# State-space rows kept in the natural order of channels, with two stores a unit

## The chip, the cores and the metric

The kernel runs on one core of one Trainium2 chip. The metric is the device time of one execution in microseconds (us). The core has five engines with queues of their own: TensorE (PE) for matrix products, ScalarE (ACT) for exponentials, VectorE (DVE) for element-wise work, GpSimd (POOL), and SyncE (SP), which in this kernel issues nearly all the transfers between DRAM and the on-chip memory (SBUF). TensorE writes its results into a small memory of its own, PSUM.

## What is computed

Two branches read the same `x` (2048 positions by 512 channels) and are mixed position by position by a gate:

```python
g = sigmoid((x * gate_w).sum(-1, keepdims=True))
# a: attention, 32 heads of 16 channels
qkv = (x @ wqkv) -> q, k, v
p = softmax(q @ k.T * 16 ** -0.5)          # 32 heads, 2048 x 2048 each
a = (p @ v) @ wo
# b: a state-space convolution, one filter of 2048 taps for each channel
dt = exp(log_dt); A = A_re + 1j * A_im
P = exp(dt * A * l)                         # 512 channels x 128 states x 2048 taps
K = einsum("dn,dnl,dn->dl", C, P, dt * B).real
b = causal_convolution(x, K) + x * Dskip
return g * a + (1 - g) * b
```

Inputs and output are 16-bit floats.

## The kernel before, in words

**Attention.** The scores of one head, 128 keys by 512 queries, make one tile; there are 2048 tiles. Three tiles are made at a time by matmuls into one of two PSUM buffers (`SC`). ACT takes the exponential of two or three of them (line 907) into `ET`. In some groups one tile is left to DVE, which makes an approximate exponential with integer arithmetic: four such tiles (`bits`, line 943, buffer `DZ`) and three more passes (`batch`, line 954, `DZ` and `DU`) make one "set". The products with `v` gather in the PSUM buffer `OA`; `norm_a`, `norm_b` and `norm_c` transpose and divide them on DVE (lines 978 to 997). There are 32 blocks of 64 tiles.

**State space.** The convolution is done in chunks of 64 positions. Filter tables are made on DVE, a scan over the chunks runs on DVE in two halves of the channels (`scan`, lines 1331 to 1342), and `ystage` makes the output. It works through 32 units of 16 channels, units 0 to 15 after the first half of the scan, 16 to 31 after the second. The channels are held in an order in which channel d stands next to channel d + 256. A unit adds up in the PSUM buffer `MB`, with four column strips (j) by four groups (q): one product of the scan's states with `Py`, one of the inputs `XY` with the short filters `Tt`. Four strips of 32 chunks of 64 positions lie on the 128 partitions, so one partition strip holds one channel of each group q. The DVE multiplies the sum by the gate into `Yst` (line 1415, four buffers in turn), and SP stores it to the DRAM tensor `ytd` with one transfer (line 1420). After every second unit `yread` (line 1433) is queued: a transposing transfer of 32 channel rows by 2048 positions from `ytd` into `Yl`, in which position lies on the partitions and the 512 channels, in the kernel's own order, in the row. `yloads` brings `Py` and `Tt` for up to three units ahead, again on SP.

**The final sums.** Of the 16 row groups of 128 positions, 12 have their attention part finished early (`early`), put out to DRAM and read back (`reload`, line 1556) into three buffers `AR`. `outs` waits for all the reads of `Yl` and then adds `Yl` to each `AR` on DVE, four row groups at a time (line 1565), stores the result (line 1567), and loads `Wo` once more. The last four row groups are done behind the last block: `ident` brings `Yl` into PSUM by a product with the identity matrix, `out_mm` adds the attention part to it, ACT or DVE copies the sum out, and it is stored. In `outs` and in `ident` the access patterns turn the kernel's order of channels into the natural one:

```python
PERM, NAT = [[1, 2], [2, 256]], [[256, 2], [1, 256]]
```

`PERM` reads two half rows, each with steps of two elements; `NAT` is the matching view of the natural order.

**What sets the order.** The order of instructions is made in Python before the kernel is built. `Sched` keeps a set of threads (generators) with priorities; each yields an engine and a cost, and `fill` picks, step by step, what is ready first by modelled times: every operation has a cost `c` and a delay `lat` in microseconds, and a reader of a transfer keeps a further margin of 2.4 (`DMARG`). `decide` chooses while this runs which score tiles go to DVE, from the modelled idle time of ACT and DVE and from whether the buffers of an earlier set are free; three windows of group numbers (`WIN`) say where this may be. So a changed cost or a further transfer changes the order of everything planned behind it. Every engine's queue is then carried out in that order, with waits on semaphores. `place` gives buffers their addresses by the stretches in which they live. Matmuls by a zero matrix (`wm`) are put in to keep TensorE busy (`FILL`).

Of the kernel before, what the change touches and what calls it, by code (L numbers as in the profile page):

```python
# [11 lines left out]
ALU = mybir.AluOpType  # L12

P = 128
S = 2048
D = 512
NH = 32
DH = 16
T = 64
NCH = S // T  # L20
NBLK = 16
CB = D // NBLK
# [65 lines left out]
class Prog:  # L88
# [133 lines left out]
    def dma(self, eng, fn, R=(), W=(), c=.45, lat=3.0, m=DMARG):  # L222
        if self.cap is not None:
            self.cap.append((self.dma, (eng, fn, R, W), dict(c=c, lat=lat, m=m)))
            return
        self.log.append((self.dma, self.q, (eng, fn, R, W)))
        k = self.dnext
        self.dnext = (k + 1) % NDSEM
        s = ("D", k)
        deps = self._deps(s, R, W)  # L230
        if self.dn[k]:
            deps[s] = max(deps.get(s, -1), self.dn[k])
        at = self.tm[eng]
        for s2, k2 in deps.items():
            at = max(at, self.fin[(s2, k2)] + .08)
        self.tm[eng] = at + c
        self.dn[k] += 1
        self.fin[(s, self.dn[k])] = at + c + lat
        self.marg[(s, self.dn[k])] = m
        self._record(eng, fn, deps, s, self.dn[k], R, W)  # L240
# [369 lines left out]
def record(nc, p, B, ins):  # L610
# [5 lines left out]
    sch = Sched(p)  # L616
    op, dma = p.op, p.dma
# [6 lines left out]
    def mm(out, lhsT, rhs, R, W, start=True, stop=True, pos=None, c=MM, a=512, cfg="F"):  # L624
        kw = {} if pos is None else dict(tile_position=pos)
        op("PE", lambda t: t.matmul(out(), lhsT(), rhs(), start=start, stop=stop, skip_group_check=True, **kw), R, W,  # L626
           c=c, lat=.15, a=a, cfg=cfg)
# [47 lines left out]
    idf, idb, x0n = B["idf"], B["idb"], B["x0n"]  # L675
# [334 lines left out]
    PERM, NAT = [[1, 2], [2, 256]], [[256, 2], [1, 256]]  # L1010
# [341 lines left out]
    Py, Tt, Yst, ytd, Yl = B["Py"], B["Tt"], B["Yst"], B["ytd"], B["Yl"]  # L1352
# [26 lines left out]
    def ystage():  # L1379
        def unit(u):  # L1380
            blk, hf = divmod(u, 2)
            qr, bl = divmod(blk, 4)
            sg, h, k8 = SG[qr // 2], qr // 2, blk % 8
            r, r2 = u % 3, u % 4
            yield ("AFTER", f"scan{h}")
            yield ("AFTER", "gt")
            yield ("AFTER", f"yl{u}")
            yield ("AFTER", f"xy{qr}")
            yield ("LOCK", "MB")
            ky = [(MB, 0, ('y', u))]  # L1390
            yield ("PE", .12)
            for j in range(4):
                mm(lambda j=j: MB(0, [[1, 256]], 32 * j, 32), lambda: wm(0, [[1, 32]]), lambda: wm(0, [[1, 256]]), [(wm, 0)], ky, True, False,
                   pos=(0, 32 * j), c=.11 if j == 0 else 0, a=64, cfg="C")
            for q in range(4):
                yield ("PE", .15)
                for ri in range(2):
                    for j in range(4):
                        i = 4 * q + j
                        mm(lambda q=q, j=j: MB(64 * q, [[1, 64]], 32 * j, 32),  # L1400
                           lambda ri=ri, i=i: sg(ri * SGH + CB * k8 + 16 * hf + 8 * (i % 2) + i // 2, [[2 * SGH, 32]]),
                           lambda ri=ri, i=i: Py(r * YN + ri * 16 * T + i * T, [[1, T]]),
                           [(sg, b_, (h, 'G')) for b_ in range(32)] + [(sg, "z"), (Py, r, u)], ky, False, False,
                           pos=(0, 32 * j), c=.075 if j == 0 else 0, a=16, cfg="C")
            for q in range(4):
                yield ("PE", .09)
                for j in range(4):
                    par, k = j % 2, 2 * q + j // 2
                    mm(lambda q=q, j=j: MB(64 * q, [[1, 64]], 32 * j, 32),
                       lambda k=k, par=par: B[f"XY{qr}"](16 * bl + 8 * hf + k, [[64, 32]], 64 * par, 64),  # L1410
                       lambda k=k, par=par: Tt(r * 512 + 64 * k, [[1, 64]], 64 * par, 64),
                       [(B[f"XY{qr}"], par), (Tt, (r, par, k // 4), u)], ky, False, True, pos=(64 * par, 32 * j), c=.085 if j == 0 else 0, a=8,
                       cfg="H")
            yield ("DVE", .4, -1)
            op("DVE", lambda v: v.tensor_tensor(Yst(r2 * 256, [[64, 4], [1, 64]]), MB(0, [[64, 4], [1, 64]]), B["gt"](0, [[0, 4], [1, 64]]),
                                                ALU.mult), ky + [(B["gt"], j) for j in range(4)], [(Yst, r2, u)], c=.37)
            sch.unlock("MB")
            sch.mark(f"yu{u}")
            yield ("SP", .45)
            dma("SP", lambda e: e.dma_start(ytd.dram(16 * u * S, [[T, P], [4 * S, 4], [1, T]]), Yst(r2 * 256, [[64, 4], [1, 64]])),  # L1420
                [(Yst, r2, u)], [(ytd, u)], c=.6, lat=3.2)
            if hf == 1:
                if bl == 3:
                    sch.mark(f"yq{qr}")
                sch.add(yread(blk), 3)

        for u in range(2 * NBLK):
            yield from unit(u)

    def yread(blk):  # L1430
        yield ("AFTER", "yu15")
        yield ("SP", 1.2)
        dma("SP", lambda e: e.dma_start_transpose(Yl(CB * blk, [[D, 16], [1, CB]]), ytd.dram(CB * blk * S, [[S, CB], [1, S]])),
            [(ytd, 2 * blk), (ytd, 2 * blk + 1)], [(Yl, blk)], c=1.26, lat=1.6)
        sch.mark(f"yr{blk}")


    def xload(b, qr):
# [120 lines left out]
    def outs():  # L1559
        for blk in range(NBLK):  # L1560
            yield ("AFTER", f"yr{blk}")
        for qc in range(3):
            AO = B[f"AR{qc}"]
            yield ("DVE", 2.3, 0)
            op("DVE", lambda v, qc=qc, AO=AO: v.tensor_tensor(AO(0, [[D, 4]] + NAT), AO(0, [[D, 4]] + NAT), Yl(4 * D * qc, [[D, 4]] + PERM), ALU.add),  # L1565
               [(AO, r, "a") for r in range(4)] + [(Yl, x) for x in range(NBLK)], [(AO, r, "y") for r in range(4)], c=2.2)
            later("SP", .5, 3, lambda qc=qc, AO=AO: dma("SP", lambda e: e.dma_start(dap(ins["out"], 512 * qc * D, [[D, P], [P * D, 4], [1, D]]), AO(0, [[D, 4], [1, D]])),
                                                        [(AO, r, "y") for r in range(4)], [(B["d_out"], qc)], c=.5, lat=3))
        yield ("SP", .5)
        wo_load(B["Wo"])  # L1570
        sch.mark("outs")
# [101 lines left out]
    def ident(i):  # L1673
        b, off, sl = banks[i]
        lt = 12 + i
        mm(lambda: b(off, NAT), lambda: idb(0, [[1, P]]), lambda: Yl(lt * D, PERM), [(idb, 0)] + [(Yl, x) for x in range(NBLK)],
           [(b, sl, ('o', lt))], True, False)

    def ahead_of(i):
# [132 lines left out]
```

## Time and profile before

| | |
|---|---|
| median of 3 runs | 839.67 us (838.98 to 843.0) |
| the profiled execution | 841.1 us, its span 839.3 us |
| ACT busy | 818.9 us |
| DVE busy | 788.4 us |
| PE busy | 696.9 us |
| mean granted TensorE clock | 0.983 of full speed |

The span runs from the first to the last instruction. "PE" is a matmul, "PEld" the load of its weights. A row of a group has the line, the engine, the operation, the tiles written and read with their shapes and the count, then the busy time in us and the mean duration of one in ns, then the idle time of the engine just before and who ended it. Durations of neighbouring instructions on one engine can overlap a little, so busy time over count is a little less than the mean duration. A row in order of time has the start, the duration in us, the engine, the line, the operation, and in brackets the idle time before it and what ended that. SPq stands for the issue of a transfer on SP's queue; the time until its data have landed is given apart.

### The profile page before, as it was taken

The page shows a single profiled execution, that of the slowest core. Times are in us where ns is not written, and L with a number is a line of the kernel's source. Part 1 is how long each engine was busy: PE and PEld are TensorE (multiplying, and loading weights), DVE is VectorE, ACT ScalarE, POOL GpSimd, SP SyncE. Part 2 cuts the span into 40 slices and gives each one's busy share as a digit, 9 for nine tenths or more (in the row PEclk, how much of TensorE's full clock was granted, in tenths as well). Part 3 has the DMA queues.
Part 4 walks back from the last instruction along what each step waited for, and adds up shares of the span by engine and source line. Part 5 has one row for each costly group of instructions (what it writes and reads, how often), then busy time and mean ns, then how long its engine had stood idle before and what let it go on. Part 6 is the DMA issues. An engine that isn't in the chain of part 4 may idle for free.

```text
span 839.3 us, 21027 instructions
## 1 busy us (share of the span) xinstructions
PE 696.9 (83%) x8977; PEld 253.4 (30%) x9002; DVE 788.4 (94%) x1344; ACT 818.9 (98%) x695; POOL 11.0 (1%) x13
## 2 busy tenths in 40 slices
PE   7787777778778888887787888789887889999987
PEld 3232332222212333332232332244432223444322
DVE  5799999998899999999999999999999989999996
ACT  7999999999999999999999999999999999999986
POOL 4000000000000000000000000000000000000000
PEclk9999999998999999999999999999999999999989
DMA  9650044792450789983392692066664025555113
GB/s 206 148 78 11 23 76 98 198 228 56 135 174 5 213 108 219 138 207 65 137 149 38 97 176 46 1 146 164 168 147 125 4 74 112 124 131 135 28 40 98
DMA packets 247954, 94.91 MB, mean 113 GB/s; under 512 B 222644, under 2 KB 234804, under 8 KB 245812
## 3 DMA queue, kind: packets, MB, share of 16 engines
q1 hardware_dynamic: 245988, 92.51, 50.1%
q10 hardware_dynamic: 1872, 1.05, 0.6%
q8 instruction: 71, 1.16, 0.5%
q14 instruction: 23, 0.19, 0.1%
HBM read 33.08 MB, written 35.01 MB: 81 GB/s over the span
## 4 chain that ended last, share of the span: by engine, by line
ACT 91%; PE 5%; DVE 2%; DMA 1%; issue 0%; ACTq 0%; DVEq 0%
ACT ET L907 91%; PE SC L626 2%; PE OA L626 2%; DMA Wk<-in_A_wqkv_dram 1%; DVE DZ L943 1%; PE MB L626 0%; DVE DZ L954 0%; DVE AR L1565 0%; DVE OT L978 0%; ACTq L630 0%; DVE Kst L1272 0%; DVE ON L990 0%; DVE OnT L997 0%; DVE KT L716 0%; DVE fo L1776 0%
## 5 line engine op out<-in xcount | busy, mean ns | idle before, releaser
L907 ACT ACTIVATE ET<-SC 128x1536 bf16<-128x1536 f32 (+1 forms) x683 | 810.6, 1545 | 8.4 <-PE SC L626 6.6
L626 PE MATMUL SC<-Qm,KT 32*128 32x512 bf16 x2048 | 279.1, 389 | 124.0 <-ACT ET L907 107.4
L626 PE MATMUL OA<-wm 128*32 128x512 bf16 (+3 forms) x1390 | 205.8, 369 | 1.2 <-DVE wm L679 1.2
L626 PE MATMUL OA<-ET,VE 128*32 128x512 bf16 x1792 | 180.8, 396 | 2.0 <-DVE OT L978 1.0
L943 DVE TENSOR_SCALAR DZ<-SC 128x512 uint16<-128x512 f32 x256 | 170.1, 683 | 9.5 <-PE SC L626 7.9
L626 PEld LDWEIGHTS SC<-Qm,KT 32*128 32x128 bf16 x2048 | 71.2, 91 | 341.5 <-ACT ET L907 300.6
L626 PEld LDWEIGHTS OA<-ET,VE 128*32 128x32 bf16 x1792 | 45.7, 93 | 104.0 <-issue 98.1
L626 PEld LDWEIGHTS OA<-wm 128*32 128x32 bf16 (+2 forms) x1390 | 55.3, 96 | 26.4 <-issue 17.7
L954 DVE TENSOR_SCALAR DZ<-DZ 128x2048 uint16<-128x2048 uint16 x64 | 44.0, 688 | 4.2 <-PE OA L626 4.1
L1304 DVE TENSOR_SCALAR SG<-MB 128x512 bf16<-128x512 f32 x64 | 43.6, 682 | 0.6 <-PE MB L626 0.2
L954 DVE TENSOR_SCALAR DU<-DZ 128x2048 uint16<-128x2048 uint16 x64 | 43.4, 686 | 0.1
L626 PE MATMUL MB<-X,Qt 128*128 128x64 bf16 x512 | 43.0, 244 | 0.0
L1339 DVE TENSOR_TENSOR G<-s,s 128x512 f32<-128x512 f32 x60 | 41.2, 687 | 1.0
L1331 DVE TENSOR_TENSOR s<-G,MU 128x512 f32<-128x512 f32 x60 | 41.1, 685 | 0.0
L1333 DVE TENSOR_TENSOR s<-G,MU 128x512 f32<-128x512 f32 x60 | 41.0, 683 | 0.0
L1336 DVE TENSOR_TENSOR s<-s,SG 128x512 f32<-128x512 f32 x60 | 40.9, 682 | 0.0
L626 PEld LDWEIGHTS MB<-X,Qt 128*128 128x128 bf16 x512 | 28.8, 116 | 20.3 <-issue 20.3
L1001 DVE TENSOR_TENSOR ft<-FP,L 128x1024 f32<-128x1024 f32 (+1 forms) x32 | 34.5, 1084 | 0.2
L1001 DVE TENSOR_TENSOR PT<-tt,tt 128x1024 bf16<-128x1024 bf16 x48 | 32.8, 683 | 0.5
L626 PEld LDWEIGHTS MB<-Py,SG 128*32 128x32 bf16 x1024 | 27.9, 167 | 6.4 <-issue 3.7
L626 PE MATMUL MB<-Py,SG 128*32 128x64 bf16 x1024 | 28.8, 231 | 0.0
L1342 DVE CAST SG<-G 128x512 bf16<-128x512 f32 x60 | 25.4, 423 | 1.2
(167 smaller groups left out, 607.7 us busy)
## 6 DMA issues: line engine op xcount, KB each, us to landing
gm_ptd<-PT SPq DMA_DIRECT2D x16, 1024.0 KB, 5.9
Py<-gm_ptd SPq DMA_DIRECT2D x32, 512.0 KB, 4.6
gm_kpd<-Kst SPq DMA_DIRECT2D x16, 256.0 KB, 3.8
Tt<-gm_kpd SPq DMA_DIRECT2D x128, 32.0 KB, 3.3
gm_xrd<-in_A_x_dram SPq DMA_DIRECT2D x1, 2048.0 KB, 13.4
gm_xcd<-wm SPq DMA_DIRECT2D x4, 512.0 KB, 10.3
gm_xcd<-XR SPq DMA_DIRECT2D x32, 64.0 KB, 1.9
Wo<-in_A_wo_dram SPq DMA_DIRECT2D x4, 512.0 KB, 4.2
```

Of the source, the lines that this page charges most:

```text
L626: op("PE", lambda t: t.matmul(out(), lhsT(), rhs(), start=start, stop=stop, skip_group_check=True, **kw), R, W, c=c, lat=.15, a=a, cfg=cfg)
L907: op("ACT", lambda a: a.activation(ET(512 * e, [[1, 512 * n]]), sc(0, [[1, 512 * n]]), AF.Exp, scale=DH ** -0.5), [(sc, i, g) for i in ran ...
L943: op("DVE", lambda v: v.tensor_scalar(z.u16(512 * k, [[1, 512 * n]]), sc(512 * na, [[1, 512 * n]]), XS, XB, ALU.mult, ALU.add), [(sc, na + ...
L954: op("DVE", lambda v: v.tensor_scalar(t.u16(0, [[1, 2048]]), z.u16(0, [[1, 2048]]), float(STEP[k][0]), None, ALU.add), R, W, c=.07 + 2048 ...
L1001: op(eng, lambda v: v.tensor_tensor(o(), a(), b_(), f), R, W, c=c)
L1304: op("DVE", lambda v, kh=kh, part=part: v.tensor_scalar(sg(2 * SGH + SGH * part + CB * k8 + 16 * kh, [[2 * SGH, 32], [1, 16]]), MB(0, [[16 ...
L1331: op(e, lambda v: v.tensor_tensor(s2(0, W), G(0, W), MU(d0, [[0, 2], [1, 256]]), ALU.mult), key("G", "MU"), [(s2, 0)], c=F5)
L1333: op(e, lambda v: v.tensor_tensor(s3(0, W), G(256, [[-256, 2], [1, 256]]), MU(D + d0, [[D, 2], [1, 256]]), ALU.mult), key("G", "MU") + [(M ...
L1336: op(e, lambda v, so=so: v.tensor_tensor(s2(0, W), s2(0, W), sg(so, [[SGH, 2], [1, 256]]), ALU.add), [(s2, 0)] + ks, [(s2, 0)], c=F5)
L1339: op(e, lambda v: v.tensor_tensor(G(0, [[1, 512]]), s2(0, [[1, 512]]), s3(0, [[1, 512]]), ALU.add), [(s2, 0), (s3, 0)], [(G, 0)], c=F5)
L1342: op(e, lambda v, so=so: v.tensor_copy(sg(so, [[SGH, 2], [1, 256]]), G(0, W)), key("G"), ks if c < NCH - 2 else [(sg, k, (h, 'G')) for k i ...
```

## The change

The tiles j of a unit are assigned to the column strips in another order, so that the two strips on the first 64 partitions hold channels of the lower half (0 to 255) and the two on the other 64 partitions channels of the upper half. Each unit is stored with two transfers of 64 partitions each, into rows of `ytd` that are in the natural order of channels. The reads into `Yl` move the same amounts, but are queued after every second pair of units, two at a time: 32 rows of the lower half and 32 rows of the upper half, each of which waits for the stores of four units. `Yl` then holds the channels in natural order, and the three additions of `outs` and the four products of `ident` use unit steps. The planner's cost of an addition goes from 2.2 to 1.14, that of its step from 2.3 to 1.2; each of the two stores keeps the cost that the one had.

```diff
 (ystage, the products of a unit)
-                        i = 4 * q + j
+                        i = 4 * q + 2 * (j % 2) + j // 2
...
-                    par, k = j % 2, 2 * q + j // 2
+                    par, k = j // 2, 2 * q + j % 2
...
-            yield ("SP", .45)
-            dma("SP", lambda e: e.dma_start(ytd.dram(16 * u * S, [[T, P], [4 * S, 4], [1, T]]), Yst(r2 * 256, [[64, 4], [1, 64]])),
-                [(Yst, r2, u)], [(ytd, u)], c=.6, lat=3.2)
+            for par in range(2):
+                yield ("SP", .45)
+                dma("SP", lambda e, par=par: e.dma_start(ytd.dram((256 * par + 8 * u) * S, [[T, 64], [2 * S, 4], [1, T]]), Yst(r2 * 256, [[64, 4], [1, 64]], 64 * par, 64)),
+                    [(Yst, r2, u)], [(ytd, (u, par))], c=.6, lat=3.2)
             if hf == 1:
                 if bl == 3:
                     sch.mark(f"yq{qr}")
-                sch.add(yread(blk), 3)
+                if blk % 2:
+                    sch.add(yread(blk - 1), 3)
...
     def yread(blk):
         yield ("AFTER", "yu15")
-        yield ("SP", 1.2)
-        dma("SP", lambda e: e.dma_start_transpose(Yl(CB * blk, [[D, 16], [1, CB]]), ytd.dram(CB * blk * S, [[S, CB], [1, S]])),
-            [(ytd, 2 * blk), (ytd, 2 * blk + 1)], [(Yl, blk)], c=1.26, lat=1.6)
-        sch.mark(f"yr{blk}")
+        for par in range(2):
+            yield ("SP", 1.2)
+            dma("SP", lambda e, par=par: e.dma_start_transpose(Yl(256 * par + 16 * blk, [[D, 16], [1, CB]]), ytd.dram((256 * par + 16 * blk) * S, [[S, CB], [1, S]])),
+                [(ytd, (2 * blk + u, par)) for u in range(4)], [(Yl, blk + par)], c=1.26, lat=1.6)
+            sch.mark(f"yr{blk + par}")
...
 (outs)
-            yield ("DVE", 2.3, 0)
-            op("DVE", lambda v, qc=qc, AO=AO: v.tensor_tensor(AO(0, [[D, 4]] + NAT), AO(0, [[D, 4]] + NAT), Yl(4 * D * qc, [[D, 4]] + PERM), ALU.add),
-               [(AO, r, "a") for r in range(4)] + [(Yl, x) for x in range(NBLK)], [(AO, r, "y") for r in range(4)], c=2.2)
+            yield ("DVE", 1.2, 0)
+            op("DVE", lambda v, qc=qc, AO=AO: v.tensor_tensor(AO(0, [[1, S]]), AO(0, [[1, S]]), Yl(S * qc, [[1, S]]), ALU.add),
+               [(AO, r, "a") for r in range(4)] + [(Yl, x) for x in range(NBLK)], [(AO, r, "y") for r in range(4)], c=1.14)
...
 (ident)
-        mm(lambda: b(off, NAT), lambda: idb(0, [[1, P]]), lambda: Yl(lt * D, PERM), [(idb, 0)] + [(Yl, x) for x in range(NBLK)],
+        mm(lambda: b(off, [[1, D]]), lambda: idb(0, [[1, P]]), lambda: Yl(lt * D, [[1, D]]), [(idb, 0)] + [(Yl, x) for x in range(NBLK)],
```

## The prediction

> **What bounds the kernel now.** I read the head of the page first (span, busy shares, the chain that ended last), then the groups of instructions kept apart by shape, then the order of time on DVE, ACT and PE around the three lines that change, and last SP's own order in the stage that stores the state-space rows.
>
> ```profile
> span 839.3 us, 21027 instructions
> ...
> PE 696.9 (83%) x8977; PEld 253.4 (30%) x9002; DVE 788.4 (94%) x1344; ACT 818.9 (98%) x695; POOL 11.0 (1%) x13
> ...
> ACT 91%; PE 5%; DVE 2%; DMA 1%; issue 0%; ACTq 0%; DVEq 0%
> ...
> L907 ACT ACTIVATE ET<-SC 128x1536 bf16<-128x1536 f32 (+1 forms) x683 | 810.6, 1545 | 8.4 <-PE SC L626 6.6
> ```
>
> ACT bounds it: the 683 exponentials fill 810.6 of 839.3 us, and ACT stands idle ahead of them for only 8.4 us in all. So there are three ways to move the end: fewer tiles on ACT, less of those 8.4 us, or a shorter stretch behind the last exponential. DVE at 94% is the second engine; it takes some of the score tiles off ACT. What one such set of four tiles is worth comes from the groups by shape, first those of ACT, then those of DVE:
>
> ```profile
> L907 ACT ACTIVATE ET<-SC 128x1536 bf16<-128x1536 f32 x426 | 583.5, 1764 | 4.0 <-PE SC L626 2.7 <-PE OA L626 1.2
> L907 ACT ACTIVATE ET<-SC 128x1024 bf16<-128x1024 f32 x257 | 250.5, 1182 | 4.4 <-PE SC L626 4.0 <-PE OA L626 0.2
> ```
>
> ```profile
> L943 DVE TENSOR_SCALAR DZ<-SC 128x512 uint16<-128x512 f32 x256 | 170.1, 683 | 9.5 <-PE SC L626 7.9
> ...
> L1339 DVE TENSOR_TENSOR G<-s,s 128x512 f32<-128x512 f32 x60 | 41.2, 687 | 1.0
> ...
> L1001 DVE TENSOR_TENSOR PT<-tt,tt 128x1024 bf16<-128x1024 bf16 x48 | 32.8, 683 | 0.5
> ...
> L1565 DVE TENSOR_TENSOR AR<-AR,Yl 128x2048 bf16<-128x2048 bf16 x3 | 6.8, 2281 | 0.0
> ```
>
> An exponential of three tiles takes 583.5/426 = 1.370 us of the engine, one of two tiles 250.5/257 = 0.975 us: a tile taken off ACT saves 0.395 us. 256 tiles are on DVE, four to a set, so 64 sets; one set more or less is 4 x 0.395 = 1.58 us of ACT.
>
> **The change, part by part.**
>
> *The three final additions (L1565).* They stay three, on the same bytes, with unit steps in place of steps of two. The price of now is in the row: 2281 ns. The same kind of operation in float takes 687 ns for 512 elements, so an element at that rate costs (2281 - 687)/(2048 - 512) = 1.04 ns, and about 156 ns are fixed. The only two-byte additions of this kernel that read in runs of neighbours, those into PT, take 683 ns for 1024 elements: (683 - 156)/1024 = 0.515 ns, twice the rate. For 2048 elements this gives 156 + 2048 x 0.515 = 1.21 us. The bounds are 2.28 us (nothing gained) and 1.21 us; I take 1.21, since the PT row has the operation, the type and the access. That frees 3 x 1.07 = 3.2 us of DVE.
>
> The Trainium skill says the same from another side: in "VectorE: DVE Perf Modes", section "Side-by-side: where the cycles go for N=2048 bf16", such an operation takes about 2293 ns at one element a cycle and about 1224 ns at two, and two need 16-bit tensors with a step of one. The trace agrees with its first figure (2281 ns); the second would free 3 x 1.06 = 3.2 us too.
>
> What of it lies on the path is seen in the order of time, first DVE, then ACT, then PE, then the busy time and granted clock (the 1.00, 0.71, 0.50 after the engines) by stretches:
>
> ```profile
> 806.88 2.28 DVE L1565 TENSOR_TENSOR AR<-AR,Yl 128x2048 bf16<-128x2048 bf16 x1
> 809.07 0.71 DVE L978 STREAM_TRANSPOSE OT<-OA 128x512 f32<-128x512 f32 x1
> 809.71 0.65 DVE L943 TENSOR_SCALAR DZ<-SC 128x512 uint16<-128x512 f32 x1
> ...
> 814.82 2.28 DVE L1565 TENSOR_TENSOR AR<-AR,Yl 128x2048 bf16<-128x2048 bf16 x1
> ...
> 817.62 2.28 DVE L1565 TENSOR_TENSOR AR<-AR,Yl 128x2048 bf16<-128x2048 bf16 x1
> ```
>
> ```profile
> 811.87 2.06 ACT L907 ACTIVATE ET<-SC 128x1024 bf16<-128x1024 f32 x2 [1.54 <-PE SC L626]
> 814.17 1.02 ACT L907 ACTIVATE ET<-SC 128x1024 bf16<-128x1024 f32 x1 [0.24 <-PE SC L626]
> 815.70 15.22 ACT L907 ACTIVATE ET<-SC 128x1024 bf16<-128x1024 f32 x13 [0.51 <-PE SC L626]
> ```
>
> ```profile
> 810.42 0.39 PE L626 MATMUL SC<-Qm,KT 32*128 32x512 bf16 x1 [1.15 <-DVE DZ L943]
> ```
>
> ```profile
> 808.00:810.00 2.00, 0.97 (x13) 0.26 (x10) 2.00 (x3) 2.00 (x3) 0.00 (x0) 1.00 0.00 0
> 810.00:812.00 2.00, 1.57 (x10) 0.42 (x11) 1.93 (x6) 0.46 (x2) 0.00 (x0) 0.71 0.79 262
> 812.00:814.00 2.00, 2.00 (x12) 0.31 (x8) 1.68 (x3) 1.92 (x2) 0.00 (x0) 0.50 0.00 0
> ```
>
> The first addition holds back the transpose of OA and the DZ behind it on DVE's queue. PE waits 1.15 us for that DZ before it can fill SC again, ACT waits 1.54 us for PE, and TensorE falls to half its clock just then. At half clock ACT waits twice more, 0.24 and 0.51 us. So 2.29 us of ACT's idle time hang on this place. Of the 1.54 us the shorter addition takes 1.07; PE's gap falls to about 0.1 us, with which I let the half clock and its 0.75 us go as well: -1.82 us. The ends for this term are 0 (the plan puts the addition in front of another score tile) and -2.29. The other two additions lie in stretches where ACT runs on from 815.70 without a gap, so their 2 x 1.07 us are worth nothing on the path unless the planner spends them on another set.
>
> On the clock, the Trainium skill, "TensorE: Matmul & The Clock Gate", Part 1, has the clock halved after at least one idle window of about 3.4 us. The trace differs: the drop comes behind a gap of 1.15 us, in two microseconds with PE busy for 0.97. By that rule the gap would not be the cause, the 0.75 us would stay, and the term would be -1.07.
>
> *Thirty-two more stores on SP, and the regrouped reads.* Rows of the Yl and Yst tiles, of SP's waits, of SP's order in the first half of the state-space output, of the scan that its second half waits for, and of SP's last issues:
>
> ```profile
> L1433 SPq DMA_TRANSPOSE Yl<-gm_ytd x16: 1202/1276/2142, 622.5 to 799.3; - x16
> ...
> DMA to landing us min/median/max: 2.4/2.6/4.3
> ```
>
> ```profile
> L1420 SPq DMA_DIRECT2D gm_ytd<-Yst x32: 394/597/1598, 547.6 to 797.4; - x32
> ```
>
> ```profile
> SPq L1433 <- DMA gm_ytd<-Yst: 1.5, 1, 1.5
> ```
>
> ```profile
> 591.03 0.60 SPq L1420 DMA_DIRECT2D gm_ytd<-Yst  x1
> 591.67 0.58 SPq L1366 DMA_DIRECT2D Tt<-gm_kpd  x1
> ...
> 593.89 0.60 SPq L1420 DMA_DIRECT2D gm_ytd<-Yst  x1
> ```
>
> ```profile
> L1339 DVE TENSOR_TENSOR G<-s,s x60: 670/691/694, 401.6 to 686.9; 128x512 f32<-128x512 f32 x60
> ```
>
> ```profile
> 641.48 1.74 SPq L1556 DMA_DIRECT2D AR<-gm_od  x2
> 650.16 1.71 SPq L735 DMA_DIRECT2D Qm<-gm_qd  x4
> ```
>
> ```profile
> 783.62 2.83 SPq L735 DMA_DIRECT2D Qm<-gm_qd  x4
> 786.55 1.23 SPq L1433 DMA_TRANSPOSE Yl<-gm_ytd  x1
> 789.57 8.22 SPq L1420 DMA_DIRECT2D gm_ytd<-Yst  x2
> 799.28 1.22 SPq L1433 DMA_TRANSPOSE Yl<-gm_ytd  x1
> ...
> 817.54 0.51 SPq L630 DMA_DIRECT2D Wo<-in_A_wo_dram  x1
> ```
>
> 32 x 0.60 = 19.2 us more on SP. In units 0 to 15 SP issues almost without a break, so there I count all of 16 x 0.60 = 9.6 us as delay of that half. What hides it: the second half waits for the scan, which ends at 687, while SP has issued the first half's loads and reads by 643 and then only a few Qm transfers (650.16). A slip to 653 has 34 us of cover. If that cover were gone, ACT would not see it either until the additions, the only readers of these rows. The other risk is a Qm load, which is in front of the scores, queued behind a second store: 0.60 us later, against a landing that the plan keeps its own margin for; 0 us, bounded by 0 and 0.60 a block.
>
> In the second half SP has room (8.2 us for the last two stores, nearly all waiting for PE and DVE), so the pace of units 16 to 31 stays. At its end the last store costs 0.40 to 0.60 more, and the last pair now leaves two transposes together where the earlier one had been issued at 786.55: 1.28 more. The last landing moves from 799.28 + 2.6 = 801.9 to about 803.7; the first addition began at 806.88, so 3.2 us of cover remain, and 0 on the path. A read that waits for four units instead of two holds the Py, Tt and Qm loads behind it on SP. All reads together waited 1.5 us before; I count no more, since the planner issues it only when it holds the stores for landed. The bounds for store and read order together are 0 and +1.9 us, all behind the last unit. Should the additions end 1.9 us later, the load of Wo behind them at 817.54 is next to be late; it lands 4.2 us after its issue and is first used at 826.20 (the two rows below), so 4.4 us of cover remain.
>
> ```profile
> Wo<-in_A_wo_dram SPq DMA_DIRECT2D x4, 512.0 KB, 4.2
> ```
>
> ```profile
> 826.20 0.10 PEld L626 LDWEIGHTS MB<-Wo,OnT 128*128 128x128 bf16 x1 [0.23 <-issue]
> ```
>
> ```profile
> L626 PE MATMUL SC<-Yl,idb x3: 388/388/399, 831.4 to 834.2; 128*128 128x512 bf16 x3
> ```
>
> *TensorE.* The same matmuls run in another order of tiles; the four sums with Yl read and write in unit steps. They take 388 ns, no more than the 0.39 us of the matmul at 810.42, which reads and writes 512 columns in unit steps already: 0.
>
> **Sum.** -1.07 - 0.75 + 0 + 0 = -1.82 us on a span of 839.3, whose run took 841.1 us, 1.4 above the median of the three. On the median: 839.67 - 1.8 = **837.9 us**. The measurement tells about 0.5% (4.2 us) from no change, so this counts as no change.
>
> **Rivals.** All of them come from one fact: the order of all engines is planned anew from the first store (547.6 us) on, with three cheaper additions and 32 more transfers.
>
> *More sets.* With 3.2 us of DVE free near the end, and the set buffers free earlier, the planner starts further sets. Two give -1.82 - 2 x 1.58 = -5.0, **834.7**; three 833.1. For it: behind the scan the planner starts a set whenever its buffers are free. Against it: a set takes more than the 3.2 us freed (4 x 0.683 for DZ alone), and the last stretch is short. It decides from two sets on.
>
> *No gain.* The additions stay at 2.28 us because the access misses the double rate, or another DVE operation stands in front of the DZ and the gap forms again: **839.7**. The PT row speaks against the first; the second is open.
>
> *More stalls (slower).* The three additions become ready together, nearer to the last blocks. Where one lands just ahead of a DZ, PE idles over a microsecond and the half clock follows, as in the rows at 810; each such place cost 2.29 us. At present one in three does it. If all three do, it costs 2 x 2.29 = +4.6: **844.3**. For it: DVE is busy in all of 808 to 810 (2.00 of 2.00), so a DZ behind an addition finds no slack. Against it: an addition of 1.21 us holds a DZ half as long. It decides from two more places on.
>
> **Chances.** Forecast 0.36, by its own terms (0 to -2.29, a set more or less beside) 836 to 840; more sets 0.27; no gain 0.10; more stalls 0.27. Thus faster 0.27, same 0.46, slower 0.27. The range runs from three sets more to three stalls, 833.0 to 844.5.
>
> **What would show it.** Right: L1565 at about 1210 ns, 64 stores at L1420 of some 0.6 us, the scan's last row still near 687, no wait of ACT for SC and no half clock near 810, and 256 tiles at L943 (264 for two more sets). Wrong: ACT's idle total above 8.4 us, new half-clock stretches, Qm loads that SC waits for, or fewer tiles at L943.

## The result

The changed kernel takes 846.87 us (median of 6 runs, 845.31 to 849.18), the kernel before 841.07 us (6 runs, 838.98 to 843.0): a ratio of 1.0072, with a 95% interval of 1.0054 to 1.009. It became slower by some 6 us, where 837.9 was forecast and 844.5 was the end of the range. The forecast started from the 839.67 us of the first three runs of the kernel before; so 1.4 of the 9.0 us between forecast and result are that starting point.

The page of the changed kernel (its profiled run took 846.18 us), the head, the chain's shares and the exponentials:

```profile
span 844.4 us, 21124 instructions
...
ACT 84%; DVE 6%; PE 5%; DMA 2%; issue 0%; SPq 0%; ACTq 0%; DVEq 0%
...
L907 ACT ACTIVATE ET<-SC 128x1536 bf16<-128x1536 f32 (+1 forms) x683 | 808.9, 1549 | 12.0 <-PE SC L626 9.1
```

ACT still bounds the kernel, but its share of the chain went from 91% to 84%. ACT has 1.7 us less to do (808.9 against 810.6) and stands idle 3.6 us longer ahead of its exponentials (12.0 against 8.4). (Neighbouring exponentials overlap by more than a little: 808.9/683 = 1.18 us of the engine each, where the mean duration is 1.549 us. The busy time is what counts.) To see where, ACT in order of time; first the kernel before in the first half of the state-space output and at the end (its last exponentials, from 815.70 on, stand in the prediction), then the changed one:

```profile
588.45 53.17 ACT L907 ACTIVATE ET<-SC 128x1536 bf16<-128x1536 f32 x43
```

```profile
834.17 0.58 ACT L1774 CAST fo<-MB 128x512 bf16<-128x512 f32 x1 [3.25 <-PE MB L626]
```

```profile
603.51 1.02 ACT L907 ACTIVATE ET<-SC 128x1024 bf16<-128x1024 f32 x1 [1.36 <-PE SC L626]
605.03 3.21 ACT L907 ACTIVATE ET<-SC 128x1024 bf16<-128x1024 f32 x3 [0.49 <-PE SC L626]
608.39 9.59 ACT L907 ACTIVATE ET<-SC 128x1536 bf16<-128x1536 f32 x8 [0.16 <-PE SC L626]
620.27 1.03 ACT L907 ACTIVATE ET<-SC 128x1024 bf16<-128x1024 f32 x1 [2.29 <-PE SC L626]
621.48 2.90 ACT L907 ACTIVATE ET<-SC 128x1536 bf16<-128x1536 f32 x2 [0.18 <-PE SC L626]
624.72 26.61 ACT L907 ACTIVATE ET<-SC 128x1536 bf16<-128x1536 f32 x21 [0.34 <-PE SC L626]
...
805.07 27.52 ACT L907 ACTIVATE ET<-SC 128x1024 bf16<-128x1024 f32 x27
...
837.98 0.58 ACT L1777 CAST fo<-MB 128x512 bf16<-128x512 f32 x1 [5.39 <-PE MB L626]
```

Three things stand in these rows. The stall near 811 that the prediction was about is gone: ACT runs from 805.07 to the last exponential without a gap. Between 602 and 625, where ACT had run without a gap, it now stands still for 1.36 + 0.49 + 0.16 + 2.29 + 0.18 + 0.34 = 4.82 us. And the work behind the last exponential got longer: that one ends at 805.07 + 27.52 = 832.59 (before: 815.70 + 15.22 = 830.92), so 11.8 us follow it in place of 8.4. The end of the exponentials moved by 1.7 us (3.6 more idle, 1.7 less work, and 0.2 us of small differences) and the tail grew by 3.4, together the 5.1 by which the spans differ. So the tail is the larger part; 2.1 us of its growth lie ahead of the first copy of the output (5.39 against 3.25), the other 1.3 behind it.

What ACT waited for in the first half: the changed kernel's chain of work that ended last around the longest gap, then SP and PE in order of time there.

```profile
613.56 0.62 SPq L1421
614.22 4.91 DMA Py<-gm_ptd
619.17 0.52 PE MB L626 x16
619.69 0.54 PE SC L626 x3
...
624.72 101.89 ACT ET L907 x91
```

```profile
612.89 1.29 SPq L1421 DMA_DIRECT2D gm_ytd<-Yst  x2
614.22 0.61 SPq L1360 DMA_DIRECT2D Py<-gm_ptd  x1
614.88 2.59 SPq L1366 DMA_DIRECT2D Tt<-gm_kpd  x4
```

```profile
619.17 0.52 PE L626 MATMUL MB<-Py,SG 128*32 128x64 bf16 x16 [2.34 <-DMA Py<-gm_ptd]
619.63 0.61 PE L626 MATMUL SC<-Qm,KT 32*128 32x512 bf16 x3
```

A second store now stands on the chain itself. The `Py` of a unit is queued behind the stores of an earlier one. It was issued at 614.22 and landed 4.91 us later; PE stood before the product with `Py` for 2.34 us, took up the next score tiles only behind it (619.63), and ACT had nothing to do. Two stores take 1.29 us of SP's queue where one took 0.64 (0.60 and the gap to the next row, 591.03 to 591.67).

The additions, the stores and the issue of `Wo` of the changed kernel, and the chain at its end:

```profile
L1568 DVE TENSOR_TENSOR AR<-AR,Yl x3: 1218/1219/1220, 826.8 to 829.1; 128x2048 bf16<-128x2048 bf16 x3
```

```profile
L1421 SPq DMA_DIRECT2D gm_ytd<-Yst x64: 595/617/1571, 547.4 to 816.8; - x64
```

```profile
826.88 1.15 DVE AR L1568
828.04 0.42 SPq L1570
828.51 5.50 DMA Wo<-in_A_wo_dram
834.06 0.82 PE MB L626 x3
```

The additions have their price, 1219 ns. But the last store left at 816.8 instead of 797.4, the additions stand side by side at 826.8 to 829.1 instead of 806.9 to 817.6, and `Wo`, queued behind the first of them, is issued at 828.51 instead of 817.54 and is now on the chain.

### The profile page after: what moved, and what is told of

Its sections match the earlier page's. It is cut to its first block, busy times and chain, and to the rows that moved or that the text cites. A ratio compares the mean times of both kernels' runs of the same rounds, so it can differ in the third digit from the quotient of the medians.

```text
span 844.4 us, 21124 instructions
## 1 busy us (share of the span) xinstructions
PE 700.8 (83%) x9018; PEld 254.4 (30%) x9018; DVE 788.2 (93%) x1350; ACT 817.2 (97%) x695; POOL 11.0 (1%) x13
## 4 chain that ended last, share of the span: by engine, by line
ACT 84%; DVE 6%; PE 5%; DMA 2%; issue 0%; SPq 0%; ACTq 0%; DVEq 0%
ACT ET L907 84%; PE SC L626 2%; DVE DZ L943 2%; PE OA L626 2%; PE MB L626 1%; DMA Wk<-in_A_wqkv_dram 1%; DMA Wo<-in_A_wo_dram 1%; DVE DZ L954 1%; DMA Py<-gm_ptd 1%; DVE s L1331 1%; DVE G L1339 0%; DVE DU L954 0%; DVE Yst L1415 0%; DVE s L1333 0%; DVE SG L1342 0%
## 5 line engine op out<-in xcount | busy, mean ns | idle before, releaser
L907 ACT ACTIVATE ET<-SC 128x1536 bf16<-128x1536 f32 (+1 forms) x683 | 808.9, 1549 | 12.0 <-PE SC L626 9.1
L943 DVE TENSOR_SCALAR DZ<-SC 128x512 uint16<-128x512 f32 x260 | 172.0, 682 | 10.9 <-PE SC L626 9.5
L954 DVE TENSOR_SCALAR DZ<-DZ 128x2048 uint16<-128x2048 uint16 x65 | 44.5, 684 | 3.8 <-PE OA L626 3.8
L954 DVE TENSOR_SCALAR DU<-DZ 128x2048 uint16<-128x2048 uint16 x65 | 43.8, 684 | 0.1
L626 PEld LDWEIGHTS MB<-Py,SG 128*32 128x32 bf16 x1024 | 28.8, 167 | 10.8 <-issue 4.8
L626 PE MATMUL OA<-DZ,VS 128*32 128x512 bf16 x260 | 25.6, 384 | 1.3 <-DVE DZ L954 1.3
```

The lines of the kernel that those rows point to most:

```text
L907: op("ACT", lambda a: a.activation(ET(512 * e, [[1, 512 * n]]), sc(0, [[1, 512 * n]]), AF.Exp, scale=DH ** -0.5), [(sc, i, g) for i in ran ...
L943: op("DVE", lambda v: v.tensor_scalar(z.u16(512 * k, [[1, 512 * n]]), sc(512 * na, [[1, 512 * n]]), XS, XB, ALU.mult, ALU.add), [(sc, na + ...
L954: op("DVE", lambda v: v.tensor_scalar(t.u16(0, [[1, 2048]]), z.u16(0, [[1, 2048]]), float(STEP[k][0]), None, ALU.add), R, W, c=.07 + 2048 ...
```

## Experiments

Each run was timed against the kernel before on the same chip; ratios are to it. Kernels whose addresses are written out have line numbers 15 lower from there on (L892 for the exponentials, L611 for the matmuls, L1345 for the loads of `Py`, L1405 or L1406 for the stores, L1550 to L1552 for the additions).

**The stores alone.** The kernel before, its old order of channels and its slow additions kept, with only the store cut into two halves of 64 partitions:

```diff
-            yield ("SP", .45)
-            dma("SP", lambda e: e.dma_start(ytd.dram(16 * u * S, [[T, P], [4 * S, 4], [1, T]]), ...
+            for par in range(2):
+                yield ("SP", .45)
+                dma("SP", lambda e, par=par: e.dma_start(ytd.dram((16 * u + 2 * par) * S, [[T, 64], [4 * S, 4], [1, T]]), ...
```

> The kernel before with one part of the change alone: each unit is stored with two transfers of 64 partitions, in the old order of channels; reads, additions and sums as before. Theory (SP's queue is too full): slower than before by 4 to 9 us, so 845 to 850 against 841.1; TensorE waits over 2 us for Py loads before 640 us, the last store comes more than 10 us later than 797 us. Rival (the three unit-step additions, put side by side late, make the loss): within 2 us of before. Rival (any re-made plan costs some us): anywhere from -3 to +6 us, without a wait for Py.

852.22 us, 1.0135 (1.0118 to 1.0152), above the band that was expected. The stores alone cost more than the whole change; PE waits 3.2 us for `Py`, ACT's idle time ahead of exponentials between 595 and 628 is 5.6 us, the last store leaves at 819.8, and the first copy behind the exponentials waits 8.79 us. But the addresses had changed as well, which costs something by itself: the last experiment below repeats this one without that.

**The additions alone.** The kernel before with only the additions in unit steps and their new cost; three quarters of the output then get their state-space part at the wrong channels:

```diff
-            yield ("DVE", 2.3, 0)
-            op("DVE", lambda v, qc=qc, AO=AO: v.tensor_tensor(AO(0, [[D, 4]] + NAT), AO(0, [[D, 4]] + NAT), Yl(4 * D * qc, [[D, 4]] + PERM), ALU.add),
+            yield ("DVE", 1.2, 0)
+            op("DVE", lambda v, qc=qc, AO=AO: v.tensor_tensor(AO(0, [[1, S]]), AO(0, [[1, S]]), Yl(S * qc, [[1, S]]), ALU.add),
```

> The kernel before with the three additions alone in unit steps (on rows that are still in the kernel's own order of channels, so the first three quarters of the output have their state-space part at wrong channels); stores, reads and last sums as before. By the term of the prediction: -1.8 us with bounds 0 and -2.3, so 838.8 to 841; additions of 1.21 us, ACT's waits of 1.54, 0.24 and 0.51 us near 811 smaller or gone. Rival (additions make the loss): 845 or more.

838.31 us, 0.9961 (0.9948 to 0.9975): 3.2 us less than the 841.48 of the kernel before beside it. Its rows: the additions, ACT in order of time, and busy times by stretches at the place of the old stall.

```profile
L1565 DVE TENSOR_TENSOR AR<-AR,Yl x3: 1201/1207/1214, 805.5 to 812.6; 128x2048 bf16<-128x2048 bf16 x3
```

```profile
799.68 26.97 ACT L907 ACTIVATE ET<-SC 128x1024 bf16<-128x1024 f32 x26
```

```profile
808.00:810.00 2.00, 1.71 (x25) 0.45 (x21) 2.00 (x4) 2.00 (x4) 0.00 (x0) 1.00 0.61 214
810.00:812.00 2.00, 2.00 (x25) 0.50 (x25) 2.00 (x3) 2.00 (x3) 0.00 (x0) 1.00 0.00 0
```

The stall and the half clock are both gone (the clock is 1.00 in both stretches). So the gain that the prediction saw exists, and it is larger than said.

**One store, natural order kept.** The changed kernel, with the old assignment of tiles to strips and one store a unit; the natural order is made by the reads, which take every second row:

```diff
-            dma("SP", lambda e, par=par: e.dma_start_transpose(Yl(256 * par + 16 * blk, [[D, 16], [1, CB]]), ytd.dram((256 * par + 16 * blk) * S, [[S, CB], [1, S]])),
-                [(ytd, (2 * blk + u, par)) for u in range(4)], [(Yl, blk + par)], c=1.26, lat=1.6)
+            dma("SP", lambda e, par=par: e.dma_start_transpose(Yl(256 * par + 16 * blk, [[D, 16], [1, CB]]), ytd.dram((32 * blk + par) * S, [[2 * S, CB], [1, S]])),
+                [(ytd, 2 * blk + u) for u in range(4)], [(Yl, blk + par)], c=1.26, lat=1.6)
```

> The changed kernel with the extra stores taken out: natural order of channels, unit-step additions and sums, reads in pairs, but one store a unit as before; the reads take every second row of the DRAM tensor instead. Theory (SP's queue): no wait of TensorE for Py, last store near 797 us, time 838 to 841 against 841.1 before and 846.9 changed. Rival (additions): it stays near 846. Rival (grouping of the reads): it stays above 843 with late additions.

845.3 us, 1.0052 (1.0036 to 1.0068): still slower than before and outside the expected 838 to 841, though no wait of PE for `Py` is left, the last store left at 803.7 and the additions took 1215 ns. Its loss is elsewhere. These are its first transposes into `XR`, near 100 us, and ACT in the stage behind them:

```profile
L1457 SPq DMA_TRANSPOSE XR<-gm_xrd x16: 1188/1208/2394, 112.1 to 186.3; - x16
```

```profile
168.04 1.45 ACT L907 ACTIVATE ET<-SC 128x1536 bf16<-128x1536 f32 x1 [3.69 <-PE SC L626]
170.11 10.85 ACT L907 ACTIVATE ET<-SC 128x1536 bf16<-128x1536 f32 x8 [0.62 <-PE SC L626]
```

In the kernel before the first of them is issued at 99.7. The order planned for this stage is the same, but `place` had given 140 of 141 tiles other addresses, and `XR` the one of `Wk`, which PE reads late: the first transpose leaves 12.5 us later, and ACT then runs dry. The next run takes just this away. (In the changed kernel the first of them leaves at 100.0, so this loss is not part of its 6 us.)

**The same with the old addresses.** The kernel of the last run with every tile at the address that it has in the kernel before (a table in place of the search in `place`):

```diff
-    best, seed = None, 1
-    for k in range(400):
...
+    for b in sbs:
+        b.lo = AT[b.name]
```

> The kernel of the one-store run, same order of all instructions, with every SBUF buffer at the address it has in the kernel before (there the buffer XR had been put over Wk, whose last readers it waited for near 100 us). Theory (the one-store run lost its time to that placement alone): ACT's wait of 3.7 us near 168 us goes, time 837 to 840, as with the additions alone (838.3). Rival (natural order or the reads in pairs cost something themselves): 843 or more.

838.33 us, 0.9974 (0.9963 to 0.9985). This beats both kernels. With the last run 3.8 us above the kernel before and this one 2.6 below, 6.4 us had been a matter of addresses alone. ACT, in the stretch in which it stalled for 4.82 us with two stores:

```profile
589.55 51.59 ACT L892 ACTIVATE ET<-SC 128x1536 bf16<-128x1536 f32 x42
```

**Thirty-two transfers more in a fixed order.** That kernel with each store cut in two, the second half planned at a cost of 0: all other instructions keep their order on every engine, and every tile its address.

```diff
-            dma("SP", lambda e: e.dma_start(ytd.dram(16 * u * S, [[T, P], [4 * S, 4], [1, T]]), Yst(r2 * 256, [[64, 4], [1, 64]])),
-                [(Yst, r2, u)], [(ytd, u)], c=.6, lat=3.2)
+            for par in range(2):
+                dma("SP", lambda e, par=par: e.dma_start(ytd.dram((16 * u + 2 * par) * S, [[T, 64], [4 * S, 4], [1, T]]), Yst(r2 * 256, [[64, 4], [1, 64]], 64 * par, 64)),
+                    [(Yst, r2, u)], [(ytd, (u, par))], c=(.6, 0)[par], lat=3.2)
```

> The kernel of the pinned one-store run with each store cut into two transfers of 64 partitions, the second one planned at no cost, so that all engines' orders and all addresses stay the same and only 32 transfers are added. Theory (SP's queue is full in units 0 to 15, each further transfer delays the Py and Tt loads that TensorE waits for): 4 to 8 us slower than the pinned one-store run, waits of TensorE for Py or Tt before 630 us of 3 us or more. Rival (SP has room, the loss came from the re-made plan): within 1.5 us of it.

847.88 us, 1.0085 (1.007 to 1.01): 9.55 us more than with one store, above the 4 to 8 that were expected. Its waits, and the last gaps of ACT in that half:

```profile
ACT ET L892 <- PE SC L611: 13.5, 18, 2.0
...
PE MB L611 <- DMA Py<-gm_ptd: 3.2, 3, 1.2
...
PE MB L611 <- DMA Tt<-gm_kpd: 2.7, 5, 1.3
```

```profile
623.70 2.79 ACT L892 ACTIVATE ET<-SC 128x1536 bf16<-128x1536 f32 x2 [2.03 <-PE SC L611]
627.95 1.45 ACT L892 ACTIVATE ET<-SC 128x1536 bf16<-128x1536 f32 x1 [1.46 <-PE SC L611]
```

The issue of one load of `Py`, first with one store a unit, then of the same load with two:

```profile
610.24 0.57 SPq L1345 DMA_DIRECT2D Py<-gm_ptd  x1
```

```profile
622.36 0.61 SPq L1345 DMA_DIRECT2D Py<-gm_ptd  x1
```

Here nothing but the transfers differs, so the first mechanism is shown: the extra issues make `Py` and `Tt` late, PE waits for them, and ACT for PE. The lateness is one of the queue and not of the transfers themselves: from issue to landing a `Py` takes 4.6 us (median; 4.5 with one store), but its issue falls behind from load to load, from 1.3 us near 545 to 12.1 us here. ACT stands still for 8.3 us between 595 and 630. The tail is as long as before (the first copy waits 3.14 us), so it is not the transfers as such that lengthen it.

**SP's real costs told to the planner.** The changed kernel, two stores and all, with three costs set to what the traces show from one issue to the next:

```diff
-            [(ptd, blk)], [(Py, r, u)], c=.62, lat=3.8)
+            [(ptd, blk)], [(Py, r, u)], c=.68, lat=4.2)
-                    [(kpd, blk)], [(Tt, (r, par, a), u)], c=.64, lat=2.8)
+                    [(kpd, blk)], [(Tt, (r, par, a), u)], c=.66, lat=2.8)
-                    [(Yst, r2, u)], [(ytd, (u, par))], c=.6, lat=3.2)
+                    [(Yst, r2, u)], [(ytd, (u, par))], c=.66, lat=3.2)
```

> The changed kernel, two stores a unit, with the planner's costs set nearer to what SP took: store 0.66 for 0.60, Py 0.68 (landing 4.2) for 0.62 (3.8), Tt 0.66 for 0.64. Theory (the loss is TensorE's in-order wait for loads that the plan holds for landed): the plan puts the units of the first half later, TensorE's waits for Py and Tt mostly go, and the time falls to 838 to 841. Rival (32 more transfers cost their time in any order): 845 or more.

841.11 us, 1.0003 (0.9987 to 1.002), at the upper end of what was expected: 5.8 us of the changed kernel's loss came back. ACT in the first half, and its exponentials behind the last store (799.8 us):

```profile
589.02 51.74 ACT L907 ACTIVATE ET<-SC 128x1536 bf16<-128x1536 f32 x42
```

```profile
L907 ACT ACTIVATE ET<-SC 128x1024 bf16<-128x1024 f32 (+1 forms) x29 | 30.4, 1208 | 1.0 <-PE SC L626 1.0
```

So with this plan two stores a unit run without the stalls of the first half and without the long tail. Unit 15 was planned later here (its `Yst` begins at 633.9, even behind the changed kernel's 629.0) and nobody waited for it: by itself a late first half cost nothing. That the told costs did this, and not merely another plan, is not shown; the run after next shows how far plans differ. A gain over the kernel before is still not left: PE waits once for a `Tt`, 1.4 us in the second half, and ACT stands still for 2.1 us around it, between 759 and 765.

**`Wo` earlier.** The changed kernel with the last load of `Wo` queued ahead of the last stores:

```diff
+        yield ("AFTER", "yu29")
+        yield ("SP", .5)
+        wo_load(B["Wo"])
...
-        yield ("SP", .5)
-        wo_load(B["Wo"])
```

> The changed kernel with the load of Wo for the last four row groups queued ahead of the last units' stores, instead of behind the first of the late additions. Theory (of the changed kernel's loss some 3 us come from that load landing at 834 us): 843 to 844.5 against 846.9. Rival (the tail is set by the last score tiles anyway): 846 to 847.5.

846.5 us, 1.007 (1.0054 to 1.0085), no better than the changed kernel. The first copy waits 4.21 us instead of 5.39, and the chain at the end goes from the last exponential through DVE instead of through `Wo`. About a third of the tail's growth, 1.2 of 3.4 us, hung on this load; the median shows next to none of it (846.5 against 846.87), with ACT's waits for the score tiles at 9.8 us in this run (one of 4.6) against 9.1. The load alone is not the loss.

**A plan made anew, with no store added.** The kernel before, one store and old additions, with only the planner's cost of the product into `Yst` raised by 0.02, and with addresses at which `XR` lies on nothing in use:

```diff
-                                                ALU.mult), ky + [(B["gt"], j) for j in range(4)], [(Yst, r2, u)], c=.37)
+                                                ALU.mult), ky + [(B["gt"], j) for j in range(4)], [(Yst, r2, u)], c=.39)
```

> The kernel before with nothing changed but the planner's cost of the gate product, 0.39 for 0.37; one store a unit and the old additions. Its plan ends the second half of the units as late as the changed kernel's does (the load of Wo last of all). Addresses are set so that XR waits for nobody. Theory (a late end of the units costs by itself, with or without more stores): 843 to 847 against 841.5, the gap between the last exponential and the first copy of the output above 5 us instead of 3.2. Rival (only the stores cost): 840 to 842.5.

848.97 us, 1.0104 (1.0088 to 1.012), above the expected 843 to 847. A change that adds no transfer and no operation costs 8 us. Its exponentials behind the last store (816.5 us), its waits, and its chain at the end:

```profile
L892 ACT ACTIVATE ET<-SC 128x1024 bf16<-128x1024 f32 (+1 forms) x13 | 14.4, 1494 | 0.0
```

```profile
PE MB L611 <- DMA Py<-gm_ptd: 3.4, 3, 1.9
```

```profile
825.84 6.60 DVE AR L1550 x3
832.44 0.61 DVE DZ L939
```

```profile
833.10 0.62 PE L611 MATMUL OA<-DZ,VS 128*32 128x512 bf16 x4 [2.60 <-DVE DZ L939]
```

The same two losses as in the changed kernel. With one store a unit, PE waits for `Py` here too, and ACT stands still for 4.3 us between 588 and 621; so late loads need no second store, a plan that orders the units otherwise can make them as well. But the exponentials end at 830.2 us, 0.7 earlier than in the kernel before: what this run lost stands behind them. These rows also show how a late end costs time. The three additions, which wait for the last rows, become ready together and stand on DVE's queue ahead of the last passes over `DZ`, and PE waits for these before its last products with `v`. In the changed kernel the shorter additions stand at the same place (826.80 to 830.29, a pass over `DZ` at 830.20), with `Wo` behind the first of them. The changed kernel's row for the same stretch (behind its last store at 816.8), and that of the kernel before (behind 797.4):

```profile
L907 ACT ACTIVATE ET<-SC 128x1024 bf16<-128x1024 f32 (+1 forms) x15 | 16.6, 1470 | 0.0
```

```profile
L907 ACT ACTIVATE ET<-SC 128x1024 bf16<-128x1024 f32 (+1 forms) x30 | 32.0, 1202 | 2.4 <-PE SC L626 2.3
```

The count of exponentials behind the last store tells an order from a delay. It is 29 or 30 in the kernel before and in the runs with the additions alone, one store, one store with the old addresses, transfers in a fixed order, and SP's real costs; there the first copy waits 3.1 to 3.25 us. It is 13 to 15 in the changed kernel, in this run, in that with `Wo` early and in that with the stores alone; there it waits 4.2 to 10.6. The late end is an order that the planner chose, not a queue that ran late: in the fixed order the last store slipped to 808.2 us, but still had 30 exponentials behind it. Which of the planner's choices leads there stays open.

**One store and real costs together**, at the addresses of the run with the real costs and two stores:

```diff
-            [(ptd, blk)], [(Py, r, u)], c=.62, lat=3.8)
+            [(ptd, blk)], [(Py, r, u)], c=.68, lat=4.2)
...
-                [(Yst, r2, u)], [(ytd, u)], c=.6, lat=3.2)
+                [(Yst, r2, u)], [(ytd, u)], c=.66, lat=3.2)
```

> The changed kernel with one store a unit (the natural order kept by reads that take every second row) and with the planner told SP's measured costs (store 0.66, Py 0.68 with a delay of 4.2, Tt 0.66), at the addresses of the kernel that had two stores and the same costs. Theory (the loss is a matter of SP's queue against the plan, and both remedies attack the same loss): they do not add up, 836 to 839 us, no wait of PE for Py or Tt, last additions of 1215 ns near 810 to 817, and the gain over the kernel before stays the additions' 2 to 4 us. Rival (two stores still cost something that the told costs do not hide): clearly below 841.1 minus 3, and below the 838.3 of one store alone: 834 to 836. Rival (told costs only shift waits): 840 or more.

839.63 us, 0.9977 (0.9965 to 0.9989). The remedies do not add up, which fits one common loss; but at 839.6 it lies just above the band that was expected, and one wait for `Py` of 1.6 us remained, with 2.14 us of gaps on ACT at 615 to 621. Of the two rivals, the one with 840 or more missed by 0.4 us, which is within the interval (838.1 to 840.1). With the told costs such waits are thus not impossible.

**The stores alone, `XR` at a good address.** The first experiment's kernel with the addresses of the changed kernel:

```diff
-    best, seed = None, 1
-    for k in range(400):
...
+    for b in sbs:
+        b.lo = AT[b.name]
```

> The kernel before with its store cut in two halves, as in the first experiment (852.2 us), but at the addresses of the changed kernel, in which the tile XR lies on nothing that is still in use. Theory: part of the first experiment's loss was XR's address (SP waited 7.3 us near 100 us of the span), and the rest is SP's full queue in the first half of the units and the late end: 845 to 849, with waits of PE for Py or Tt and additions of 2.28 us behind 820 us. Rival (the store alone makes all of it): 851 to 853. Rival (addresses make all of it): 839 to 842.

849.01 us, 1.0096 (1.0078 to 1.0114), at the upper end of the first theory's band. The loss went from 10.7 to 7.9 us, so 2.8 us of the first experiment's were its addresses. The rest is the two losses again: PE waits 4.3 us for a `Py`, ACT shows a gap of 4.40 us at 623, the additions of 2285 ns stand at 829.6 to 834.1, and the first copy waits 6.70 us.

## Why the prediction was wrong

*The price of an addition* was right: 1219 ns measured for 1.21 us forecast. The Trainium skill's figure for two elements a cycle ("VectorE: DVE Perf Modes", section "Side-by-side: where the cycles go for N=2048 bf16"), 1224 ns, agrees as well.

*The gain of the additions* had the right mechanism and too small a size. The sum had -1.07 for the shorter addition and -0.75 for the half clock. With the additions alone the kernel is 3.2 us faster. All 2.29 us of the idle time near 811 went, which was the far end given for this term, since PE's gap closed wholly and was not left at 0.1 us; what the other 0.9 us are is not settled. The clock behaved as the term said at that place: the gap went and the half clock with it. In the changed kernel it is 0.58 and then 0.50 in the stretches around the gap of 2.34 us, and the score matmuls behind it take 0.61 us in place of 0.39:

```profile
616.00:618.00 2.00, 0.67 (x12) 0.20 (x8) 2.00 (x5) 1.99 (x3) 0.00 (x0) 1.00 0.93 240
618.00:620.00 2.00, 0.83 (x19) 0.49 (x19) 0.33 (x1) 0.00 (x0) 0.00 (x0) 0.58 1.02 175
620.00:622.00 2.00, 2.00 (x39) 0.97 (x36) 1.69 (x3) 1.54 (x2) 0.00 (x0) 0.50 0.51 83
```

By the Trainium skill, "TensorE: Matmul & The Clock Gate", Part 1, it takes an idle window of about 3.4 us to halve the clock; the trace differs once more, with PE busy for 1.5 of the 4 us before 620. A gap of a microsecond is not needed either: the changed kernel has an earlier half-clock stretch, 601.27 to 608.10, ahead of which no single gap of PE was longer than 0.52 us; PE was busy for 2.33 of the 3.41 us before it. This stretch, the one from 618.34 and the one in the kernel before (810.84 to 817.67) each last 6.83 us.

*The stores of the first half* are the step that failed: "What hides it: the second half waits for the scan", "34 us of cover", and "ACT would not see it either". As a size the delay was near (9.6 us; unit 15's `Yst` began 10.8 us later, at 629.0 instead of 618.2), in part by luck: 490 exponentials had started by then instead of 485, so some of it was planned. In the fixed order, where only the queue can delay it, it was 11.3 us (617.8 to 629.1). The scan indeed did not mind. But the cover was sought at the readers of the rows that are stored. The one who waits stands behind the stores on the same queue: `Py` and `Tt` of the following units, and behind these PE's queue, which runs in the planned order and holds the score tiles that ACT needs. The prediction asked this of the `Qm` loads, rightly found 0 there (no wait of PE for `Qm` in the changed kernel), and named `Py` and `Tt` only behind a waiting read, not behind a second store. It had itself read that SP issues almost without a break there. Counted, this says that there was no room. From 546.8 to 618.2, 71.4 us, SP of the kernel before issued 55 `Tt`, 13 `Py`, 15 stores, 12 `Qm`, three `XY` and one `Wo`:

```profile
L1366 SPq DMA_DIRECT2D Tt<-gm_kpd x128: 573/610/1521, 487.9 to 778.0; - x128
```

```profile
L1360 SPq DMA_DIRECT2D Py<-gm_ptd x32: 570/581/1785, 486.0 to 771.1; - x32
```

With these medians, 0.60 for a store, 0.50 for a `Qm` (1.99 for four at 602.29), 0.62 for an `XY` (616.93), 0.42 for `Wo` and 0.04 from the end of one issue to the next, that is 58.4 + 99 x 0.04 = 62.3 us of 71.4. A second store for each of the 15 units, at 0.617 + 0.04, makes it 72.2. This is an estimate, but it says what the runs then showed: the queue goes from nearly full to over-full, and a lag adds up from load to load. It costs 9.55 us in a fixed order.

*"The pace of units 16 to 31 stays"* failed too. Their last `Yst` came at 815.7 instead of 797.0, by the plan's order. With it failed the cover of the `Wo` load: the prediction gave it 4.4 us against a slip of 1.9, and the slip was 11.0 (828.51 against 817.54). The cover was overstated too: 4.2 us is the median of four such loads, and the one at 817.54 took 6.2 us to land, which left 2.5 us. The prediction weighed the delay of one store and one read behind the last unit, not that of the units in a new plan.

*The reads* held nothing back that the traces show, and *TensorE* was right at 0: the products with `Yl` take 379 to 390 ns (388 to 399 before).

*The rivals.* "More stalls (slower)" had the sign, and at 844.3 a time 2.6 us too low, but not the place: the three additions did become ready together, but behind the last DZ of the score tiles (L943); they hold back the last passes over a set (L954) and lengthen the tail instead of making ACT wait. ACT's new stalls lie 200 us earlier. "More sets" came half true: 260 tiles on DVE against 256, one set, worth 1.7 us of ACT (1.58 forecast). The sum for the changed kernel, as far as the runs carry it: about -3 for the additions and about +9 for SP's full queue and the plan's late end together. How the 9 us split cannot be read off single runs, since each remedy tried changes both or makes a new plan. So it is shown that a second store delays `Py` and `Tt` and what this costs in a fixed order; why the plan of the changed kernel ends the units late stays open.

## What to carry to other kernels

Before a transfer is added to a queue, add up what the queue issues in that stage, from one issue to the next, and set it against the stage's length; then ask who stands behind the new transfer on its queue, and who stands behind that one on the next in-order engine, not only who reads its data. Where a planner orders everything, its costs should be those of the trace, above all for the resource that is nearly full, and the cost of a plan made anew for a trifle (here 8 us) belongs beside any measured difference. Keep the addresses fixed when two kernels are compared: here they alone were worth 2.8 and 6.4 us.

## What was not expected of the hardware

A store of half the size costs SP as much: 617 ns at 32 KB, 597 ns at 64 KB. Here the number of transfers counts, not their size.

The clock was granted at 0.751 on average in the profiled run of the kernel with one store and the old addresses. Its row by core:

```profile
core 0: 839.3 us, clock 0.751
```

That run took 841.09 us, the slowest of its 12 (median 838.33), so in this one execution three quarters of TensorE's clock cost some 3 us at most. Half the clock near a gap of PE is another matter: the two half-clock stretches of the changed kernel (from 601.27 and from 618.34) hold 4.3 of ACT's 4.82 us of idle time there. How much of it is the clock and how much the wait for the loads is not separated.
